# Output-weight load, down-weight splits, last value store and opening block of a fused attention and SwiGLU kernel

## The chip, the cores and the metric

The kernel runs on one core of a Trainium2 chip. The metric is the device time of one execution in microseconds. Three runs of the kernel before gave 1403.45, 1401.09 and 1399.49 us, median 1401.09 us. The profiler recorded one execution, which took 1402.34 us; its recorded span, to which every time of the trace belongs, is 1400.6 us.

## The reference

```python
def reference(A_x, A_wqkv, A_wo, B_x, B_w_gate, B_w_up, B_w_down):
    xn = _layernorm(A_x)                                   # x: [1, 2048, 512]
    q, k, v = (xn @ wqkv) as 3 x 32 heads x 16             # wqkv: [512, 1536]
    p = softmax(einsum("bhqd,bhkd->bhqk", q, k) * 16**-0.5)
    s = (p @ v) as [2048, 512] @ wo                        # wo: [512, 512]
    f = (silu(xn @ w_gate) * (xn @ w_up)) @ w_down         # 512 -> 1792 -> 512
    return A_x + s * silu(f)
```

All tensors are float32. The 2048 rows are both queries and keys, so 32 heads each need a 2048 x 2048 score matrix.

## The kernel before, in words

**Stages.** The prologue normalises x, multiplies by wqkv in four blocks of 512 rows and writes queries, keys and values to DRAM scratch (`q_d`, `k_d`, `v_d`). Its last stretch ends in a runtime branch (L801): a flag (L798) tells whether a cheap bound on the scores suffices. For the given data it does, and all five engines jump over the long general path. Then come attention with the feed-forward network (FFN) woven in, and an output projection with the final product.

**Attention.** The heads form 8 groups of 4, the queries 4 blocks of 512 rows: 32 units, each over 16 tiles of 128 keys. Keys and values of a group lie in a ring of four chunks of four tiles (`kst`, `vst`); chunks 0 and 1 have their memory before the branch, chunks 2 and 3 only after the prologue's pools are given back. PE multiplies one tile as two pairs of score matrices (L891), ACT takes their exponential (L894, L902), and one block later PE multiplies them with the values (`values`, L419). A block is a run of 2 to 6 key tiles of a unit. In some blocks, listed in `SHARED`, VectorE copies chosen half pairs out of PSUM (L899), and ACT takes their exponential from the copy at the end of the block (L912). A pair numbered n with sharing writes its second half into a PSUM bank of its own, `spare`; there is only one such bank, so each such copy has to end before the next shared pair's second half is written.

**The filling.** While ACT works, PE does FFN work in small steps, here called tokens: one token is a pair of 64-row matmuls into `bankx` and `banky` (L238). A feature tile has 24 tokens (gate with up), of which there are 7 in a group, followed by a down-projection of 4 times 21 tokens; 2 groups make a token block of 512 rows, and there are 4 of those. `fill(n)` issues n tokens behind a pair of scores. `plan()` chooses, by costs written in it, how many key tiles and how many tokens each block has, and its first entries are set by hand: `FIRST` gives the tokens ahead of the first pair and behind each pair of block 0.

**What rides on the tokens.** At a tile's first token VectorE splits the next tile's gate and up weights into two parts (`split_gu`, L198 and L199) and SP issues the loads of the tile after that. At its eighth token SP loads the tile's rows of the down weights into the only raw buffer, `wdr` (L204). At its last token VectorE forms the product (L268, L269), splits it (L230, L231), and `split_hidden` then splits the down weights (L208, L209). The output weights' rows use the same buffer `wdr` (`load_wo`, L302); the first of them is asked for at the last token of the last gate tile. SP issues its DMAs in program order: an issue that waits holds up all behind it.

**Order around the branch.** The last block of values is copied out of PSUM by ACT in four tiles (L714) into `vt` and stored to `v_d` by one DMA that SP issues behind the branch. SP then loads the ring's chunks 2 and 3, then the weights of gate tile 3 and the down weights of tile 1.

Of the kernel before, what the change touches and what calls it, by code (L numbers as in the profile page):

```python
# [25 lines left out]
NB = 4  # L26
TB = S // NB
NT = TB // P
# [11 lines left out]
DC = D // HALF  # L40
LIMIT = 160.0
SIZES = (2, 3, 4, 5, 6)
LAST = (3, 3, 3, 3, 2, 2)
FIRST = (4, 0, 4, 3, 3, 2, 2)
EARLY = 2


# [10 lines left out]
def plan():  # L58

    ends = [0]
    for i in range(2 * NB):
        nf = GROUPS[i % 2].stop - GROUPS[i % 2].start
        for n in [3 * DC] * nf + [3 * nf] * NT:
            ends.append(ends[-1] + n)

    ends = [n - ends[1] for n in ends[2:]]
    first = [(3, sum(FIRST)), (2, ends[0] - sum(FIRST))]
    units = H // 4 * NB
    start, stop = sum(k for k, _ in first), (units - 2) * KT
    pace = (ends[-1] - ends[0]) / (stop - start)
    short = lambda k, n: 15 * len(SHARED[k, n][0]) if (k, n) in SHARED else 250 * max(0, 6 * (k - 1) - n)
    ways = {at: {} for at in range(start, stop + 1)}
    ways[start][ends[0]] = 0, None
    for at in range(start, stop):
        room = KT - at % KT  # L80
        for done, (cost, _) in ways[at].items():
            rem = next((n for n in ends if n > done), done) - done
            for k in SIZES:
                for n in [rem] + list(range(3, rem - 2)):
                    to = at + k, done + n
                    if not n or n > 6 * k + 6 or k > room or room - k == 1:
                        continue
                    if abs(to[1] - ends[0] - (to[0] - start) * pace) > 45:
                        continue
                    c = cost + 327 + short(k, n) + (650 if n == rem and k == 2 else 0) + abs(n - 4.1 * k) / 2  # L90
                    if to[1] not in ways[to[0]] or ways[to[0]][to[1]][0] > c:
                        ways[to[0]][to[1]] = c, (at, done, k, n)

    rest = [3 * (DT - 1)] * EARLY
    pairs = {4: (2, 2), 5: (3, 2), 6: (3, 3)}
    cost = lambda r: ways[stop - r][ends[-1]][0] + sum(short(k, n) for k, n in zip(pairs[r], rest))
    r = min((r for r in pairs if ends[-1] in ways[stop - r]), key=cost)
    middle, step = [], ways[stop - r][ends[-1]][1]
    while step:
        middle.insert(0, step[2:])  # L100
        step = ways[step[0]][step[1]][1]
    rest += [3 * DT] * (NT * (NB - 1))
    parts = []
    for k, n in first + middle + list(zip(pairs[r] + 2 * LAST, rest)):
        m = 2 * k - 2
        even = [n // m + (i < n % m) for i in range(m)]
        shared, behind = SHARED.get((k, n), ((), even))
        parts.append((k, shared, [0, 0, *behind]))
    parts[0] = 3, (), list(FIRST[1:])
    return parts  # L110


# [1 line left out]
def tile_block(ctx: ExitStack, tc: tile.TileContext, x, wqkv, wo, w_gate, w_up, w_down, out):  # L114
# [3 lines left out]
    mm, act, dve, sp, pool = nc.tensor.matmul, nc.scalar.activation, nc.vector, nc.sync, nc.gpsimd  # L118
# [4 lines left out]
    v_d = dram.tile([NG, P, KT, VW], F32, name="v_d")  # L123
# [83 lines left out]
    def split_wd(f, i):  # L207
        dve.tensor_copy(wd[:, f, 0], wdr[i])  # L208
        dve.tensor_sub(wd[:, f, 1], wdr[i], wd[:, f, 0].bitcast(F32))  # L209
# [12 lines left out]
            after.pop(0)()  # L222


    kept = []

    def split_hidden():
        while kept:
            f, i, ga = kept.pop(0)
            dve.tensor_copy(hh[:, f, 0], ga)  # L230
            dve.tensor_sub(hh[:, f, 1], ga, hh[:, f, 0].bitcast(F32))  # L231
            split_wd(f, i)

    halves = [slice(h * HALF, (h + 1) * HALF) for h in range(2)]

# [11 lines left out]
    def ffn(b):  # L247
        for grp, part in enumerate(GROUPS):
            nf = part.stop - part.start
            for f in range(nf):  # L250
                i = b * NF + part.start + f
                if i + 1 < NB * NF:
                    split_gu(i + 1)
                if i + 2 < NB * NF:
                    load_gu(i + 2)
                hi, lo = gu.pop(i)
                n = 0
                for c in range(DC):
                    for wt, j in ((hi, 0), (hi, 1), (lo, 0)):
                        both(wt[:, c], fx[:, j, c], n == 0, n == 3 * DC - 1)  # L260
                        n += 1
                        if n == DC and i:
                            load_wd(i)
                        if n == 3 * DC:
                            th = one.tile([P, TB], F32, tag="th", name="th")
                            ga = two.tile([P, TB], F32, tag="ga", name="ga")
                            act(th, bankx, AF.Tanh, scale=0.5)  # L267
                            dve.scalar_tensor_tensor(ga, th, 1.0, bankx, op0=ALU.add, op1=ALU.mult)  # L268
                            dve.scalar_tensor_tensor(ga, ga, 0.5, banky, op0=ALU.mult, op1=ALU.mult)  # L269
                            kept.append((f, i, ga))  # L270
                            if now >= 0:
                                split_hidden()
                            if grp == 1 and f == nf - 1 and b + 1 < NB:
                                load_fx(b + 1, 0)
                                load_fx(b + 1, 1)
                            elif grp == 1 and f == nf - 1:
                                load_wo(0)
                        yield 3 * DC - n
            for t in range(NT):
                n = 0  # L280
                for f in range(nf):
                    for a, w in ((0, 0), (0, 1), (1, 0)):
                        both(hh[:, f, a, t * P:(t + 1) * P], wd[:, f, w], n == 0, n == 3 * nf - 1)
                        n += 1
                        if n == 3 * nf and grp == 0:
                            dve.tensor_copy(facc[:, t], bankx)
                            dve.tensor_add(facc[:, t], banky, facc[:, t])
                        elif n == 3 * nf:
                            y = two.tile([P, D], F32, tag="ga", name="y")
                            dve.tensor_add(y, bankx, facc[:, t])  # L290
                            dve.tensor_add(y, banky, y)
                            after.append(partial(store_gate, y, b * TB + t * P))
                            if b == NB - 1:
                                after.append(partial(next_out, t))
                        yield 3 * nf - n
# [4 lines left out]
    def load_wo(c):  # L300
        wor[c] = one.tile([P, D], F32, tag="wdr", name="wor")
        sp.dma_start(wor[c], wo[c * P:(c + 1) * P])  # L302
# [19 lines left out]
    plain, last, parts_o, lhs = [], [], {}, {}  # L322
# [156 lines left out]
    begin, n = [], 0  # L479
# [10 lines left out]
    with ExitStack() as pro:  # L490
# [74 lines left out]
        vt = plast.tile([P, NG, NT, VW], F32, name="vt")  # L565
# [120 lines left out]
        def feature_tile(b, m):  # L686
# [9 lines left out]
            if b:  # L696
                dve.tensor_max(top[m], top[m], sq)

        def value_tile(b, t):
            xh, xl = xt[b % 2]  # L700
            order = None
            if b == 0:
                parts = [slice(i, i + 1) for i in range(3)] if t == 1 else [slice(0, 3, 2), slice(1, 2)]
                order = [(i, part) for part in parts for i in range(DT)]
                if t == 1:
                    order.insert(11, (partial(turn_x, 0, 2), None))
            if b == t == 0:
                ps = first_tile()
            else:
                ps = project([(vh[:, c], vl[:, c], c) for c in range(DT)], xh, xl, slice(t * P, (t + 1) * P), order,  # L710
                             extra if b == t == NB - 1 else None)
            if b == 0 and t == 1:
                turn_x(0, 3)
            nc.scalar.copy(vt5[:, :, t, :, :DH], ps.rearrange("p (g h d) -> p g h d", g=NG, h=4))  # L714
            if t == NT - 1:
                store = partial((pool if b < NB - 1 else sp).dma_start, v_d[:, :, b * NT:(b + 1) * NT].rearrange("g p t c -> p g t c"), vt)
                if b < NB - 1:
                    store()
                return store


        def copy_fx(i):
# [78 lines left out]
        with tc.If(fast < 1):  # L801
            with tc.tile_pool(name="gen", bufs=1) as gen:
                for h in range(2):
                    pool.memset(qst[0][h * HALF:h * HALF + 2].bitcast(F32), 0.0)
                for g in range(NG):
                    for b in range(NB):
# [3 lines left out]
                        for j in range(NB):  # L810
                            load_k(g, j, j % 2)
                            for i in range(4 * NT):
                                h, t = divmod(i, NT)
# [36 lines left out]
    on = [att.tile([P, TB], F32, name=f"on{b}") for b in range(NB)]  # L850

    now = 0
    split_hidden()
    prev = None

    exps = []
# [2 lines left out]
    for u in range(units):  # L859
        g, b = divmod(u, NB)  # L860
        q = qst[u % 2]
        kt = 0
        for now in range(begin[u], begin[u + 1]):
            size, shared, parts = blocks[now]
# [4 lines left out]
            if not now:  # L869
                fill(FIRST[0])  # L870
            for n in range(2 * size):
                t, j = tiles[n // 2], n % 2
# [136 lines left out]
```

## Time and profile before

| what | before |
|---|---|
| runs, median | 1403.45, 1401.09, 1399.49 us; 1401.09 us |
| profiled execution, its span | 1402.34 us, 1400.6 us |
| PE busy | 1391.4 us (99% of the span) |
| ACT busy | 1109.6 us (79%) |
| VectorE (DVE) busy | 690.2 us (49%) |
| mean DMA rate | 107 GB/s |

A row of a timeline has the start in us, the duration in us, the engine (SPq is SP's queue of DMA issues), the line, the operation with its output and inputs, and in brackets the idle time ahead of it and what ended that. A row of the waits has the waiting instruction, what it waited for, the total in us, the number of times and the longest. A row of the windows has the window, its length, the busy time of PE, of PE's weight loads, DVE, ACT and POOL with the number of instructions, the granted TensorE clock as a share of full speed, the DMA engines' busy share and GB/s.

### The profile page before, as it was taken

Reading aid. Unit: us, or ns where it says so; the run is one execution under the profiler, and the core shown is the slowest. Engines: PE = TensorE matmul, PEld = TensorE weight load, DVE = VectorE, ACT = ScalarE, POOL = GpSimd, SP = SyncE. Lnnn points to the kernel's source line nnn. Section 1 sums busy time; section 2 is a strip of 40 time slices with the busy share of each in tenths; the row PEclk is TensorE's granted clock in tenths of the full one; section 3 lists DMA queues with packets and bytes.
Section 4 is the critical chain, followed back from the end, with each engine's and each line's share of the span. In section 5 each row is a group of like instructions: output and inputs, shape, how many; then the busy total and the mean of one; then the engine's idle time right before and its main releaser. Section 6 shows DMA issues by size and latency. Waiting matters only on the chain.

```text
span 1400.6 us, 27099 instructions
## 1 busy us (share of the span) xinstructions
PE 1391.4 (99%) x11197; PEld 832.3 (59%) x11197; DVE 690.2 (49%) x1121; ACT 1109.6 (79%) x1513; POOL 90.4 (6%) x102
## 2 busy tenths in 40 slices
PE   9999999999999999999999999999999999999998
PEld 7788655556555555565555555555555555555554
DVE  6643354254534563545356534644465435444645
ACT  6733588888888888887888888989888888878774
POOL 4200100000000000000000000000000000000254
PEclk9999999999999999999999999999999999999999
DMA  7778541134453511245524302447334212223643
GB/s 241 263 249 265 148 107 43 35 80 100 112 124 82 132 43 35 50 120 108 133 62 118 81 13 58 100 99 148 81 80 125 52 28 59 69 58 106 198 143 114
DMA packets 127648, 149.17 MB, mean 107 GB/s; under 512 B 12577, under 2 KB 79649, under 8 KB 126750
## 3 DMA queue, kind: packets, MB, share of 16 engines
q1 hardware_dynamic: 122206, 126.72, 35.8%
q0 software_dynamic: 4880, 20.12, 3.9%
q8 instruction: 90, 1.47, 0.4%
q10 hardware_dynamic: 432, 0.52, 0.1%
q14 instruction: 40, 0.33, 0.1%
HBM read 107.46 MB, written 40.11 MB: 105 GB/s over the span
## 4 chain that ended last, share of the span: by engine, by line
PE 86%; DMA 1%; DVE 1%; SPq 0%; ACT 0%; issue 0%; DVEq 0%
PE acc L419 32%; PE bankx L238 30%; PE score L891 18%; PE banky L238 6%; PE spare L891 1%; DMA wdr<-in_B_w_down_dram 1%; PE spare L947 0%; DMA kst<-k_d 0%; PE banky L947 0%; SPq L164 0%; PE score L947 0%; DVE ga L269 0%; DVE pr L899 0%; SPq L191 0%; DVE wd L208 0%
## 5 line engine op out<-in xcount | busy, mean ns | idle before, releaser
L894 ACT ACTIVATE pr<-score 128x1024 f32<-128x1024 f32 x746 | 725.6, 1028 | 101.7 <-PE score L891 90.3
L419 PE MATMUL acc<-pr,vst 128*17 128x512 f32 x4096 | 462.0, 593 | 0.0
L891 PE MATMUL score<-qst,kst 50*128 50x512 f32 x1770 | 408.3, 408 | 2.5 <-DMA kst<-k_d 2.5
L238 PE MATMUL bankx<-fx,guh 64*128 64x512 f32 x896 | 302.5, 393 | 0.1
L238 PE MATMUL banky<-fx,guh 64*128 64x512 f32 x896 | 302.2, 392 | 0.0
L891 PEld LDWEIGHTS score<-qst,kst 50*128 50x128 f32 x1770 | 195.7, 185 | 167.2 <-ACT pr L894 67.6
L419 PEld LDWEIGHTS acc<-pr,vst 128*17 128x17 f32 x4096 | 110.2, 97 | 279.8 <-issue 272.5
L899 DVE COPY pr<-spare 128x512 f32<-128x512 f32 x162 | 111.9, 690 | 247.7 <-PE spare L891 207.8
L902 ACT ACTIVATE pr<-score 128x512 f32<-128x512 f32 x219 | 130.7, 597 | 99.5 <-PE spare L891 90.0
L238 PE MATMUL bankx<-wd,hh 64*128 64x512 f32 x672 | 199.6, 396 | 0.0
L238 PE MATMUL banky<-wd,hh 64*128 64x512 f32 x672 | 199.3, 395 | 0.0
L238 PEld LDWEIGHTS bankx<-fx,guh 64*128 64x128 f32 x896 | 167.0, 187 | 28.5 <-issue 0.9
L238 PE MATMUL banky<-fx,gul 64*128 64x512 f32 x448 | 175.4, 392 | 0.0
L238 PE MATMUL bankx<-fx,gul 64*128 64x512 f32 x448 | 175.4, 392 | 0.0
L238 PEld LDWEIGHTS banky<-fx,guh 64*128 64x128 f32 x896 | 167.1, 187 | 3.9
L238 PEld LDWEIGHTS bankx<-wd,hh 64*128 64x128 f32 x672 | 126.7, 189 | 20.2
L268 DVE SCALAR_TENSOR_TENSOR ga<-th,bankx 128x512 f32<-128x512 f32 x56 | 38.5, 687 | 193.0 <-ACT th L267 193.0
L238 PEld LDWEIGHTS banky<-wd,hh 64*128 64x128 f32 x672 | 126.8, 189 | 4.1
L912 ACT ACTIVATE pr<-pr 128x512 f32<-128x512 f32 x221 | 121.1, 626 | 0.0
L891 PE MATMUL spare<-qst,kst 50*128 50x512 f32 x278 | 116.2, 418 | 0.7 <-DVE pr L899 0.6
L238 PEld LDWEIGHTS bankx<-fx,gul 64*128 64x128 f32 x448 | 83.0, 185 | 14.2
L238 PEld LDWEIGHTS banky<-fx,gul 64*128 64x128 f32 x448 | 83.0, 185 | 2.2
(171 smaller groups left out, 1402.2 us busy)
## 6 DMA issues: line engine op xcount, KB each, us to landing
gur<-in_B_w_gate_dram SPq DMA_DIRECT2D x56, 256.0 KB
gur<-in_B_w_up_dram SPq DMA_DIRECT2D x56, 256.0 KB
wdr<-in_B_w_down_dram SPq DMA_DIRECT2D x56, 256.0 KB
kst<-k_d SPq DMA_DIRECT2D x192, 64.0 KB
qst<-q_d SPq DMA_DIRECT2D x192, 64.0 KB
fx<-xt_d SPq DMA_DIRECT2D x24, 512.0 KB
q_d<-parts SPq DMA_DIRECT2D x16, 512.0 KB
k_d<-parts SPq DMA_DIRECT2D x16, 512.0 KB
```

The lines of the kernel that those rows point to most:

```text
L238: mm(bank, lhs[h], rhs[h], start=start, stop=stop)
L268: dve.scalar_tensor_tensor(ga, th, 1.0, bankx, op0=ALU.add, op1=ALU.mult)
L419: mm(acc[h * 32:h * 32 + DH + 1], v[:, kt % CT, h * (DH + 1):(h + 1) * (DH + 1)], probs[2 * i + h // 2][:, h % 2], start=kt == 0, stop=kt ...
L891: mm(spare if apart and h else room[:, h], k[r, j, kc * P:(kc + 1) * P], q[r, j], start=True, stop=True)
L894: exps.append(act(pr, room, AF.Exp, scale=0.25))
L899: dve.tensor_copy(pr[:, h], src)
L902: exps.append(act(pr[:, h], src, AF.Exp, scale=0.25))
L912: exps.append(act(part, part, AF.Exp, scale=0.25))
```

## The change

Four edits are made together.

1. `load_wo(0)` moves from the last token of the last gate tile to the eighth token of the last down-projection's first row tile.
2. The split of a tile's down weights moves out of `split_hidden` to the eighth token of the next tile (for tile 0 to the last token of tile 1, for a group's last tile to the eighth token of the down-projection that follows), and the load of the next rows goes right behind it. The product's split of tile 0, which stood at the head of the attention, moves to the end of tile 1.
3. The last block of values is stored by two DMAs: tiles 0 to 2 by one that stands ahead of the branch on SP, tile 3 by one behind it.
4. Unit 0 has blocks of 4, 6 and 6 key tiles with 20, 24 and 24 tokens, where it had 3, 2, 5 and 6 tiles with 14, 6, 24 and 24 tokens. The first of them shares pairs 4 and 7 with VectorE, the second is now of the shared kind. From unit 1 on the plan is the same.

```diff
-FIRST = (4, 0, 4, 3, 3, 2, 2)
+FIRST = (4, 0, 5, 2, 4, 1, 2, 3, 3)
...
-    first = [(3, sum(FIRST)), (2, ends[0] - sum(FIRST))]
+    first = [(4, ends[0])]
...
-    parts[0] = 3, (), list(FIRST[1:])
+    parts[0] = 4, (4, 7), list(FIRST[1:])
...
-    kept = []
+    kept, waiting = [], []
...
         while kept:
-            f, i, ga = kept.pop(0)
+            f, ga = kept.pop(0)
             dve.tensor_copy(hh[:, f, 0], ga)
             dve.tensor_sub(hh[:, f, 1], ga, hh[:, f, 0].bitcast(F32))
-            split_wd(f, i)
...
-                        if n == DC and i:
+                        if i and n == (DC if i > 1 else 3 * DC):
+                            while waiting:
+                                split_wd(*waiting.pop())
                             load_wd(i)
...
-                            kept.append((f, i, ga))
+                            kept.append((f, ga))
+                            waiting.append((f, i))
...
-                            elif grp == 1 and f == nf - 1:
-                                load_wo(0)
...
+                        if t == 0 and n == DC:
+                            split_wd(*waiting.pop())
+                            if grp == 1 and b == NB - 1:
+                                load_wo(0)
...
+        def store_v(engine, b, first, last):
+            dst = v_d[:, :, b * NT + first:b * NT + last].rearrange("g p t c -> p g t c")
+            engine.dma_start(dst, vt[:, :, first:last])
...
-            if t == NT - 1:
-                store = partial((pool if b < NB - 1 else sp).dma_start, v_d[:, :, b * NT:(b + 1) * NT].rearrange("g p t c -> p g t c"), vt)
-                if b < NB - 1:
-                    store()
-                return store
+            if b < NB - 1 and t == NT - 1:
+                store_v(pool, b, 0, NT)
+            elif b == NB - 1 and t == NT - 2:
+                store_v(sp, b, 0, t + 1)
+            elif b == NB - 1 and t == NT - 1:
+                return partial(store_v, sp, b, t, NT)
...
     now = 0
-    split_hidden()
     prev = None
```

**SP around the branch.** The program of SP has the store of the last values (`v_d<-vt`), the branch, and the end of the skipped path. Before, with the semaphores that a row waits for (the eight DMAHW ones count the landings of SP's DMAs):

```order
L798 TENSOR_LOAD flag_216 [waits DVE_49]
L798 ISA x2
L801 COMPARE_AND_BRANCH
...
L801 UNCONDITIONAL_BRANCH [waits DMAHW0_49,DMAHW1_49,DMAHW2_49,DMAHW3_49,DMAHW4_49,DMAHW5_49,DMAHW6_49,DMAHW7_49]
L833 DMA v_d_61<-vt_163 128x8x272 [waits DMAHW3_49,Activation_49]
```

And with the change:

```order
L807 TENSOR_LOAD flag_216 [waits DVE_49]
L807 ISA x2
L705 DMA v_d_61<-vt_163 128x8x204 [waits DMAHW3_49,Activation_49]
L810 COMPARE_AND_BRANCH
...
L810 UNCONDITIONAL_BRANCH [waits DMAHW0_49,DMAHW1_49,DMAHW2_49,DMAHW3_49,DMAHW4_49,DMAHW5_49,DMAHW6_49,DMAHW7_49]
L705 DMA v_d_61<-vt_163 128x8x68 [waits DMAHW4_49,Activation_49]
```

Three quarters of the store now stand ahead of the branch and wait for ACT's copy of the third value tile; the last quarter, in pieces of 68 numbers where a piece had 272, stands where the whole store stood. The wait for all eight counters of landings stands on the path that joins behind the branch; the skipped path's counts are added there too.

**VectorE in block 1 of the change.** In the rows of VectorE `pr<-spare` and `pr<-score` are the copies of shared pairs, `guh` and `gul` the split of a gate tile's weights, `wd` the split of down weights, `hh` the split of a product. Before, between the split of tile 1's product and the first copy of unit 0's last block:

```order
L230 CAST hh<-ga 128x512
L231 TENSOR_TENSOR hh<-ga,hh 128x512
L208 CAST wd<-wdr 128x512
L209 TENSOR_TENSOR wd<-wdr,wd 128x512
L198 CAST guh<-gur 128x1024
L199 TENSOR_TENSOR gul<-gur,guh 128x1024
L268 SCALAR_TENSOR_TENSOR ga<-th,bankx 128x512
```

With the change, from the same product of tile 1 on:

```order
L230 CAST hh<-ga 128x512
L231 TENSOR_TENSOR hh<-ga,hh 128x512
L907 COPY pr<-spare 128x512
L198 CAST guh<-gur 128x1024
L199 TENSOR_TENSOR gul<-gur,guh 128x1024
L907 COPY pr<-spare 128x512
L208 CAST wd<-wdr 128x512
L209 TENSOR_TENSOR wd<-wdr,wd 128x512
L907 COPY pr<-spare 128x512 x2
L907 COPY pr<-score_8967 128x512
```

The split of tile 3's weights (`guh`, `gul`) now stands between the copies of pairs 2 and 5 of the block, and the split of tile 1's down weights between those of pairs 5 and 7. The later rows of this kind are the same in every block of 6 tiles and 24 tokens that shares pairs: before, the copies of pairs 5, 7 and 9 followed each other, and the down weights were split ahead of the copy of pair 2.

**SP ahead of group 7's last key chunks.** `kst` is a key chunk, `vst` a value chunk, `wdr` the down weights' rows, `wor` the output weights'. Before:

```order
L204 DMA wdr<-in_B_w_down_dram 128x512
L302 DMA wor<-in_A_wo_dram 128x512
L164 DMA kst_8967<-k_d 16x2x512 x6
L181 DMA vst_8968<-v_d 128x272
L164 DMA kst_8971<-k_d 16x2x512 x6
```

With the change:

```order
L204 DMA wdr<-in_B_w_down_dram 128x512
L164 DMA kst_8968<-k_d 16x2x512 x6
L181 DMA vst_8969<-v_d 128x272
L164 DMA kst_8972<-k_d 16x2x512 x6
L181 DMA vst_8973<-v_d 128x272
L164 DMA qst_8976<-q_d 16x2x512 x6
L177 DMA qst_8976<-sh_d 2x2x512 x2
L306 DMA wor<-in_A_wo_dram 128x512 x2
```

The load of the output weights has gone from ahead of both chunks to behind them and behind the loads of the next unit's queries.

## The prediction

> **What bounds the kernel now.** First the page's busy times and its chain:
>
> ```profile
> PE 1391.4 (99%) x11197; PEld 832.3 (59%) x11197; DVE 690.2 (49%) x1121; ACT 1109.6 (79%) x1513; POOL 90.4 (6%) x102
> PE 86%; DMA 1%; DVE 1%; SPq 0%; ACT 0%; issue 0%; DVEq 0%
> ```
>
> PE is busy in 1391.4 of 1400.6 us. None of the edits takes a matmul away, so each can win only what PE idles (9.2 us in all) or what it runs at a low clock, and each can lose by making PE wait. Two places of the trace have such losses: the last key chunks of group 7 and the opening of the attention. The first is seen in SP's queue, its waits, and PE:
>
> ```profile
> 1226.43 0.35 SPq L204 DMA_DIRECT2D wdr<-in_B_w_down_dram  x1
> 1240.40 0.33 SPq L302 DMA_DIRECT2D wor<-in_A_wo_dram  x1
> 1240.83 2.71 SPq L164 DMA_DIRECT2D kst<-k_d  x6
> ```
> ```profile
> SPq L302 <- DVE wd L209: 11.3, 1, 11.3
> ```
> ```profile
> 1245.36 0.47 PE L891 MATMUL score<-qst,kst 50*128 50x512 f32 x1 [2.04 <-DMA kst<-k_d]
> 1246.26 0.76 PE L891 MATMUL score<-qst,kst 50*128 50x512 f32 x1 [0.43 <-DMA kst<-k_d]
> ```
>
> The output weights' load waits 11.3 us for the buffer, the key load queued behind it starts at 1240.83, and PE idles 2.04 and 0.43 us for it. The windows show what follows. First the block with this stall and one of the same size (5 tiles, 21 tokens); then the stretch of the idle time, and the next:
>
> ```profile
> 1235.82:1254.34 18.52, 16.05 (x112) 9.78 (x112) 6.14 (x11) 11.61 (x17) 0.00 (x0) 0.82 0.35 94
> 1094.40:1107.19 12.79, 12.79 (x112) 7.17 (x112) 5.60 (x9) 11.51 (x18) 0.00 (x0) 1.00 0.00 1
> ...
> 1242.32:1245.72 3.40, 1.36 (x11) 0.67 (x7) 0.59 (x1) 1.38 (x2) 0.00 (x0) 1.00 0.71 189
> 1245.73:1252.55 6.82, 6.39 (x31) 5.39 (x32) 0.37 (x1) 3.67 (x4) 0.00 (x0) 0.50 0.48 127
> ```
>
> After a stretch of 3.40 us in which PE worked 1.36 us, the granted clock is 0.50 for 6.82 us. Half a clock over 6.82 us costs about 3.4 us; with the idle 2.47 us that is nearly the 5.73 us by which the block exceeds its like. The opening is the second place: the four blocks of unit 0, then a block of 6 tiles with sharing behind one of 4, and one behind one of 6:
>
> ```profile
> 157.29:162.55 5.26, 5.26 (x42) 3.57 (x39) 0.00 (x0) 4.74 (x6) 0.03 (x1) 1.00 0.63 213
> 162.55:168.15 5.60, 5.60 (x46) 2.59 (x46) 4.88 (x6) 4.20 (x7) 4.53 (x4) 1.00 0.44 109
> 168.15:178.12 9.97, 9.97 (x87) 7.22 (x84) 4.20 (x7) 9.92 (x14) 0.00 (x0) 1.00 0.73 168
> 178.12:192.64 14.52, 13.82 (x115) 7.75 (x111) 9.87 (x15) 10.18 (x15) 0.00 (x0) 1.00 0.67 146
> 853.25:865.55 12.30, 12.30 (x106) 7.36 (x106) 7.27 (x12) 10.35 (x15) 0.00 (x0) 1.00 0.26 58
> 865.55:879.43 13.88, 13.88 (x123) 7.96 (x121) 8.71 (x13) 12.38 (x19) 0.00 (x0) 1.00 0.26 57
> ```
>
> Unit 0 takes 35.35 us (157.29 to 192.64).
>
> **The change part by part.** The sum is made against the profiled execution, 1402.34 us, and put on the median of the runs, 1401.09 us, which lies 1.25 us below.
>
> **Edit 1, output weights: -5.8 us.** With the load gone from ahead of the keys, they queue behind the last `wdr` load only. That load now waits for a split at its tile's eighth token, in the place where VectorE stood at about 1230 to 1232, so the keys start near 1232 and come some 8 us ahead of need. The block then takes what its kind takes, 12.7 to 12.8 us: 18.52 less 12.75 is 5.8. The output weights themselves are asked for after the last chunk; nothing needs them before the output projection's first split, a down-projection later. If the half clock came from something else, only 2.5 us would be won.
>
> **Edit 4, the opening, first without waits.** Block 0 has 8 pairs of scores and 20 tokens behind them (four tokens stand ahead, as before). The 6 pairs and 14 tokens of before took 5.26 us, 0.26 each; 28 of these make 7.0 to 7.3. Blocks 1 and 2 are the kinds of the last two rows above, 12.30 and 13.9 to 14.0. That is 33.3 us, 2.1 less than 35.35. To this the waits are added, and there are two.
>
> **Edit 3, the store in two parts.** SP before, and the copies by ACT that it waits for:
>
> ```profile
> 156.79 0.40 SPq L833 DMA_DIRECT2D v_d<-vt  x1
> 162.45 2.67 SPq L164 DMA_DIRECT2D kst<-k_d  x6
> ...
> 169.95 0.67 SPq L191 DMA_DIRECT2D gur<-in_B_w_gate_dram  x1
> 170.68 0.61 SPq L191 DMA_DIRECT2D gur<-in_B_w_up_dram  x1
> 171.40 0.56 SPq L204 DMA_DIRECT2D wdr<-in_B_w_down_dram  x1
> ```
> ```profile
> SPq L164 <- DMA v_d<-vt: 4.7, 1, 4.7
> SPq L801 <- SPq L801: 4.4, 1, 4.4
> ```
> ```profile
> 153.38 0.59 ACT L714 COPY vt<-ps 128x512 f32<-128x512 f32 x1 [2.40 <-PE ps L641]
> 156.18 0.59 ACT L714 COPY vt<-extra 128x512 f32<-128x512 f32 x1 [2.21 <-PE extra L641]
> ```
> ```profile
> 157.29 0.67 PE L891 MATMUL score<-qst,kst 50*128 50x512 f32 x4
> ```
>
> SP's branch costs it 4.4 us. Before, that lay beside the projection of the last value tiles: SP had nothing to do until ACT's copy ended at 156.77. Now part 1 stands ahead of the branch and waits for the third copy, 153.97. SP branches at about 154.4, is through at 157.4 (a branch of 3 us) to 158.8, and then waits on the eight counters for part 1's landing as well. The whole store took from 156.79 to 162.4 to land; three quarters of it, begun at 154.0, land between 158.2 (in proportion) and 159.6. PE's first scores wait for these counters too. So they start between 158.2 and 159.6 instead of 157.29: 0.9 to 2.3 us of idle PE, say 1.6. Part 2 is issued about 159 instead of 156.79. It holds a quarter of the bytes in as many pieces, so it lands after 1.4 us (by bytes) to 5.6 us (by pieces): at 160.4 to 164.6 where before it was 162.4. I take 163, near the middle and nearer the pieces, since the pieces are what stays the same. The prologue's memory, and with it the ring's key loads, comes free 0.5 us later rather than earlier.
>
> [...]
>
> **Who waits for that: VectorE, then PE.** The loads of tile 3's weights (169.95, 170.68) and tile 1's down weights (171.40) come behind twelve key issues, 7.5 to 9 us after the ring starts. VectorE before shows when the last of them landed and what the splits take:
>
> ```profile
> 176.38 0.43 DVE L208 CAST wd<-wdr 128x512 fp32r<-128x512 f32 x1 [4.46 <-DMA wdr<-in_B_w_down_dram]
> 176.84 0.69 DVE L209 TENSOR_TENSOR wd<-wdr,wd 128x512 fp32r<-128x512 f32 x1
> 177.45 0.69 DVE L198 CAST guh<-gur 128x1024 fp32r<-128x1024 f32 x1
> 178.17 1.23 DVE L199 TENSOR_TENSOR gul<-gur,guh 128x1024 fp32r<-128x1024 f32 x1
> ```
>
> The down weights landed at 176.38, so tile 3's, issued 0.7 us ahead of them, at about 175.5. Before, only VectorE felt this (4.46 us), for its block shared nothing. In the changed order the split of tile 3 stands ahead of the copy of pair 5, and PE may not write pair 7's second half before that copy ends. Landing 175.5 + 0.5 (later ring), splits 1.9, copy 0.7: pair 7 cannot go on before about 178.6. PE comes there 8.4 us into the block (7 pairs, 3.4 us of values, 12 tokens): at 157.29 + 7.0 + 8.4 = 172.7 without the first wait, 174.3 with it. So PE waits about 4.3 us there, and with the first wait 5.9 us in all, or 5.9 whether the first is 0.9 or 2.3, as long as the ring start is the same. Pair 9 then follows the split of the down weights closely, which adds up to 0.5. Unit 0: 33.3 + 6.2 = 39.5 us against 35.35, **+4.2 us**; with part 2's ends (160.4 or 164.6) +1.6 to +5.9.
>
> **The clock after that wait: +3.4 us.** More than 4 us without a matmul, with a stretch of 3.4 us in which PE works less than 1.36 us, is what halved the clock at 1245.73. I expect the same here: another 3.4 us, unless the first wait does it (then the slow time ends inside the second wait and costs little).
>
> [...]
>
> **Edit 2, splits beside the next tile.** VectorE and PE in one of the 26 later blocks of 6 tiles that share:
>
> ```profile
> 226.85 0.68 DVE L899 COPY pr<-spare 128x512 f32<-128x512 f32 x1
> 228.35 0.69 DVE L899 COPY pr<-spare 128x512 f32<-128x512 f32 x1 [0.82 <-PE spare L891]
> ```
> ```profile
> 229.30 0.39 PE L891 MATMUL spare<-qst,kst 50*128 50x512 f32 x1
> ```
>
> The copies of pairs 5 and 7 start at 226.85 and 228.35, with 0.82 us of idle time between; the split (0.43 and 0.69, 1.07 in a chain) now lies there. Pair 7's copy starts at 226.85 + 0.61 + 1.07 = 228.53 instead of 228.35 and ends at 229.22, 0.08 ahead of pair 9's second half at 229.30. A semaphore's way and the weight load use most of that. So nothing (0 us) to 0.1 us a block; I take 0.04, **+1.0 us** for 26. Elsewhere the moved splits fall in idle time: VectorE is busy 49%. If that cover were gone, each would cost its 1.07 us.
>
> **Sum:** -5.8 + 4.2 + 3.4 + 1.0 = +2.8 us: 1405.1 for a profiled execution like the one of before, 1403.9 on the median. I say 1404.0.
>
> **The rivals.**
> *A. The opening waits, but the late clock stays whole* (the first wait of up to 2.3 us in one stretch halves it instead, and the slow time runs into the second wait; or neither does). For: the first wait reaches 2.04 us in a third to half of its range. Against: its middle is 1.6. -5.8 + 4.2 + 1.0 = -0.6: 1400.5.
> *B. It does what it says.* Part 2 lands near 160.4 or the weights land sooner behind a less loaded queue, and PE waits for nothing in the opening: -5.8 - 2.1 + 0.5 = -7.4: 1393.7. Against it stands the twelve-issue queue ahead of tile 3's weights: even a ring start 2 us earlier only takes 2 us from a wait of 4.3.
> *C. Slower by the splits.* If pair 7's copy comes too late in each of the 26 blocks (it decides at about 0.06 us ahead of the matmul, which the rows leave open with 0.08), PE loses about 0.12 us a block and the weight load's cover: 3.1 instead of 1.0, on top of the forecast: 1406.1. For: the lead is small and the same in all 26 blocks. Against: by the rows it is just enough.
>
> **How the numbers follow.** Forecast 0.45 (1404.0, own range 1401 to 1406), A 0.31 (1400.5, from 1398 with an early part 2 to 1402), B 0.10 (1393.7), C 0.14 (1406.1, up to 1408). The range that leaves out B and the outermost ends of the others is 1397.5 to 1408. About 0.3%, 4.2 us, is what a measurement of this kernel can tell from no change: faster is below 1396.9, slower above 1405.3. Faster: B and little of A, 0.11. Slower: C and 0.2 of the forecast's upper end, 0.34. The rest, 0.55, is no change.
>
> **What would show it.** Right: no DMA wait and a clock of 1.00 near 1240; PE's first score at 158.2 to 159.6; PE waiting about 4 us for VectorE's copy (`spare`) some 8 us into block 1, behind a DVE wait for `gur`; half a clock after it; blocks of 6 shared tiles 0 to 0.1 us longer. Wrong: key loads of the ring starting before 161, no `spare` wait in block 1, or a clock of 1.00 all through 157 to 190.

## The result, and the profile after

In 20 runs of each, the changed kernel took 1402.45 us (1400.47 to 1404.90) and the kernel before 1400.53 us (1397.39 to 1403.45), both medians. The ratio is 1.0012, with a 95% interval of 1.0005 to 1.0019: 0.7 to 2.7 us slower. The forecast was 1404.0 us, by a sum of +2.8 us. The profiled execution took 1403.09 us, its span is 1401.3 us. Lines of code are numbered anew in the change: the scores are L899 now, the copies L907, the last store L705.

On the page PE works as long as before, in a span 0.7 us longer; the busy times of the other engines have moved by less than 2 us, that of the weight loads (PEld) by 7.6:

```profile
PE 1391.3 (99%) x11197; PEld 839.9 (60%) x11197; DVE 691.6 (49%) x1128; ACT 1109.4 (79%) x1517; POOL 89.5 (6%) x102
```

**Group 7's last keys.** SP's queue in the change (this part of the program runs 6.8 us later than before), and the block that took 18.52 us before:

```profile
1239.20 0.35 SPq L204 DMA_DIRECT2D wdr<-in_B_w_down_dram  x1
1239.65 4.14 SPq L164 DMA_DIRECT2D kst<-k_d  x6
...
1251.07 10.43 SPq L306 DMA_DIRECT2D wor<-in_A_wo_dram  x2
```
```profile
1242.63:1255.32 12.69, 12.69 (x112) 7.42 (x112) 6.13 (x11) 11.42 (x18) 0.00 (x0) 1.00 0.46 123
```

The keys go out right behind the `wdr` load, the output weights wait behind them, PE never idles and the clock is 1.00. The block takes 12.69 us: 5.8 us are won.

**The opening.** SP, PE's two waits, and VectorE ahead of the second of them:

```profile
154.50 5.78 SPq L705 DMA_DIRECT2D v_d<-vt  x2
163.62 2.67 SPq L164 DMA_DIRECT2D kst<-k_d  x6
...
170.07 0.67 SPq L191 DMA_DIRECT2D gur<-in_B_w_gate_dram  x1
170.78 0.63 SPq L191 DMA_DIRECT2D gur<-in_B_w_up_dram  x1
171.87 0.62 SPq L204 DMA_DIRECT2D wdr<-in_B_w_down_dram  x1
```
```profile
160.05 1.37 PE L899 MATMUL score<-qst,kst 50*128 50x512 f32 x4 [2.07 <-SPq L810]
179.22 0.50 PE L899 MATMUL spare<-qst,kst 50*128 50x512 f32 x1 [1.90 <-DVE pr L907]
```
```profile
176.62 0.69 DVE L198 CAST guh<-gur 128x1024 fp32r<-128x1024 f32 x1 [2.48 <-DMA gur<-in_B_w_up_dram]
177.34 1.23 DVE L199 TENSOR_TENSOR gul<-gur,guh 128x1024 fp32r<-128x1024 f32 x1
178.49 0.68 DVE L907 COPY pr<-spare 128x512 f32<-128x512 f32 x1
```

The row of the two stores runs from the first part's issue to the end of the second's: the branch lies in its 5.78 us. PE waits 2.07 us for SP's branch (L810): SP spends 3.9 us on the branch itself and then 0.4 us on the landing of part 1. Later VectorE waits for tile 3's weights, and the copy of pair 5, queued behind their split, ends at 179.17; PE had to have that bank free and goes on at 179.22. The windows show what each wait did to the clock (first five rows), and then the three blocks of unit 0 (last three rows):

```profile
156.92:160.33 3.41, 1.34 (x10) 0.83 (x11) 1.29 (x2) 0.34 (x1) 0.00 (x0) 1.00 0.39 118
160.34:163.75 3.41, 3.41 (x17) 3.17 (x18) 0.00 (x0) 1.94 (x2) 0.08 (x1) 0.50 0.37 84
163.76:167.16 3.40, 3.40 (x29) 2.73 (x27) 0.69 (x1) 3.08 (x4) 3.24 (x4) 1.00 0.49 110
177.40:180.81 3.41, 1.58 (x12) 1.11 (x12) 3.38 (x5) 0.90 (x3) 0.00 (x0) 1.00 0.35 99
180.82:184.23 3.41, 3.41 (x18) 2.69 (x18) 1.05 (x3) 1.96 (x3) 0.00 (x0) 0.50 1.10 223
160.05:168.63 8.58, 8.58 (x56) 7.19 (x58) 1.19 (x2) 6.49 (x8) 3.78 (x4) 0.80 0.46 108
168.63:184.83 16.20, 14.30 (x106) 8.60 (x106) 10.78 (x18) 11.02 (x16) 0.00 (x0) 0.89 0.80 176
184.83:198.99 14.16, 14.16 (x124) 8.55 (x120) 8.62 (x13) 12.28 (x19) 0.00 (x0) 1.00 0.19 47
```

Behind each wait the clock is halved for one stretch of 3.41 us. The two halved stretches begin 20.48 us apart (160.34 and 180.82), which is six times 3.41. Unit 0 ends at 198.99, before at 192.64; 0.51 us of the difference was there ahead of the opening (the third copy of values began at 153.89 instead of 153.38). The opening thus lost 5.84 us, as much as edit 1 won. So the gain of edit 1 near 1240 is there in full, and it had been given away beforehand, between 157 and 199.

### The profile page after: what moved, and what is told of

The parts are those of the page before. It is cut to its first block, busy times and chain, and to the rows that moved or that the text cites. A ratio compares the mean times of both kernels' runs of the same rounds, so it can differ in the third digit from the quotient of the medians.

```text
span 1401.3 us, 27070 instructions
## 1 busy us (share of the span) xinstructions
PE 1391.3 (99%) x11197; PEld 839.9 (60%) x11197; DVE 691.6 (49%) x1128; ACT 1109.4 (79%) x1517; POOL 89.5 (6%) x102
## 4 chain that ended last, share of the span: by engine, by line
PE 87%; SPq 0%; DMA 0%; DVE 0%; issue 0%; DVEq 0%
PE acc L423 32%; PE bankx L237 29%; PE score L899 18%; PE banky L237 7%; PE spare L899 1%; DMA gur<-in_B_w_up_dram 0%; SPq L164 0%; PE spare L955 0%; PE banky L955 0%; PE score L955 0%; DVE gul L199 0%; SPq L181 0%; DVE guh L198 0%; DVE y L962 0%; SPq L191 0%
## 5 line engine op out<-in xcount | busy, mean ns | idle before, releaser
L899 PE MATMUL score<-qst,kst 50*128 50x512 f32 x1766 | 408.8, 408 | 2.1 <-SPq L810 2.1
L899 PEld LDWEIGHTS score<-qst,kst 50*128 50x128 f32 x1766 | 195.3, 185 | 162.9 <-ACT pr L902 67.3
L907 DVE COPY pr<-spare 128x512 f32<-128x512 f32 x167 | 115.0, 689 | 257.4 <-PE spare L899 212.9
L920 ACT ACTIVATE pr<-pr 128x512 f32<-128x512 f32 x228 | 125.2, 631 | 0.0
L899 PE MATMUL spare<-qst,kst 50*128 50x512 f32 x282 | 118.8, 421 | 1.9 <-DVE pr L907 1.9
```

The source lines that it names most:

```text
L899: mm(spare if apart and h else room[:, h], k[r, j, kc * P:(kc + 1) * P], q[r, j], start=True, stop=True)
L907: dve.tensor_copy(pr[:, h], src)
L920: exps.append(act(part, part, AF.Exp, scale=0.25))
```

## The experiments

All times are medians; ratios are to the kernel before, run on the same chip beside each, with 95% intervals.

| kernel | edits in it | median us | ratio, interval |
|---|---|---|---|
| the change | 1, 2, 3, 4 | 1402.45 | 1.0012, 1.0005 to 1.0019 |
| wo_only | 1 | 1395.25 | 0.9958, 0.9945 to 0.9972 |
| one_store | 1, 2, 4 | 1402.30 | 1.0011, 1.0002 to 1.0020 |
| old_opening | 1, 2, 3 | 1399.21 | 0.9986, 0.9977 to 0.9995 |
| one_store_old_opening | 1, 2 | 1395.77 | 0.9965, 0.9953 to 0.9978 |
| early_gate | all, tile 3's weights earlier | 1398.48 | 0.9985, 0.9976 to 0.9994 |
| both_behind | all, both stores behind the branch | 1402.85 | 1.0019, 1.0010 to 1.0028 |
| weights_first | 1, 2, 4, loads in another order | 1395.28 | 0.9964, 0.9949 to 0.9978 |
| weights_first_two_parts | the same, both stores behind the branch | 1395.96 | 0.9967, 0.9956 to 0.9979 |
| wo_only_again | 1 | 1395.08 | 0.9962, 0.9948 to 0.9976 |
| weights_first_again | as weights_first | 1394.94 | 0.9959, 0.9945 to 0.9973 |

The theory: edit 1 wins 5.8 us; the opening loses them again in two waits of PE, one from the store ahead of the branch (edit 3) and one from the shared copies queued behind the split of weights that come late (edit 4), each with a stretch of halved clock. The rivals: the half clock near 1245 had another cause; or one of the two waits is only the other's consequence.

**Edit 1 alone (wo_only).**

```diff
-                            elif grp == 1 and f == nf - 1:
-                                load_wo(0)
...
+                        if t == 0 and n == DC and grp == 1 and b == NB - 1:
+                            load_wo(0)
```

> The kernel before with edit 1 alone: the output weights' load behind the last keys, all else as before. Theory: the wait of 2.5 us and the half clock that it brings both go, so the block that took 18.52 us takes 12.7, and the kernel runs 5.5 to 6 us faster than before (ratio near 0.996). Rival: the half clock there has another cause (a DMA burst, say) and stays; then only the wait of 2.5 us comes back (ratio near 0.998).

The ratio is 0.9958, so 5.9 us faster (3.9 to 7.7). The block in question, in windows of this kernel, and two stretches of its opening:

```profile
1236.98:1249.67 12.69, 12.69 (x112) 7.13 (x112) 6.14 (x11) 11.43 (x18) 0.00 (x0) 1.00 0.16 44
...
184.72:188.13 3.41, 2.02 (x17) 1.47 (x17) 2.36 (x5) 2.06 (x3) 0.00 (x0) 1.00 0.23 42
188.14:191.55 3.41, 2.84 (x26) 2.02 (x24) 2.47 (x3) 1.86 (x3) 0.00 (x0) 1.00 0.30 97
```

The block is 5.83 us shorter, with the whole clock. The rival that gave the half clock another cause is out; a burst of DMAs alone did not halve it in weights_first, below, where the DMA engines are busy 0.99 of block 0 at a clock of 1.00. The second pair of rows is of use further down: PE idled 1.39 us of a stretch here, and the clock stayed whole.

**One store (one_store): edit 3 undone.**

```diff
-            elif b == NB - 1 and t == NT - 2:
-                store_v(sp, b, 0, t + 1)
             elif b == NB - 1 and t == NT - 1:
-                return partial(store_v, sp, b, t, NT)
+                return partial(store_v, sp, b, 0, NT)
```

> The changed kernel with edit 3 undone: one store of the last values behind the branch. Theory (two waits, each with a stretch of halved clock): PE's first score comes right behind its four tokens, no clock is lost in block 0, the ring's keys start about 1.2 us earlier; the wait at pair 7 of block 1 stays and is longer, 4 to 5 us, since PE comes there earlier and the weights of tile 3 still land behind twelve key loads. Unit 0 ends 1 to 2 us earlier than with the change. Rival (the branch is what costs, the wait at pair 7 is only its consequence): with the first wait gone block 1 runs without a wait above 1 us and unit 0 ends 5 us or more earlier.

The time is that of the change (1.0011 against 1.0012). SP and PE of this kernel (its scores are L897, its copies L905), and its windows: blocks 0 and 1, then the stretches of the wait.

```profile
156.86 0.40 SPq L705 DMA_DIRECT2D v_d<-vt  x1
162.23 2.67 SPq L164 DMA_DIRECT2D kst<-k_d  x6
```
```profile
178.45 0.79 PE L897 MATMUL spare<-qst,kst 50*128 50x512 f32 x1 [5.38 <-DVE pr L905]
```
```profile
157.38:164.38 7.00, 7.00 (x58) 4.98 (x56) 1.37 (x3) 6.41 (x8) 1.97 (x3) 1.00 0.56 186
164.38:184.08 19.70, 14.31 (x107) 8.72 (x105) 11.32 (x18) 10.70 (x16) 1.98 (x2) 0.83 0.75 172
...
171.94:175.35 3.41, 1.13 (x9) 0.57 (x7) 0.00 (x0) 1.65 (x3) 0.00 (x0) 1.00 1.01 222
175.36:182.18 6.82, 3.73 (x18) 2.94 (x20) 4.42 (x7) 1.51 (x2) 0.00 (x0) 0.50 0.81 192
```

The first wait is gone and block 0 takes 7.00 us; then PE waits 5.38 us for the same copy, more than the 4 to 5 expected. It comes to that place at 173.07, with the change at 177.32: its first score is 2.67 us later there and block 0 takes 1.58 us longer. So with the change it waited less, and the second wait is no consequence of the first: it takes up the time that the first one costs. The release of the ring at 162.23 instead of 163.62 moved the copy by only 0.8 us. Unit 0 ends 0.87 us earlier than with the change, where 1 to 2 us were expected; behind this longer wait the half clock lasts 6.82 us instead of 3.41.

**The old opening (old_opening): edit 4 undone.** `FIRST` and the first blocks as before; edits 1 to 3 stay.

> The changed kernel with edit 4 undone: unit 0 in blocks of 3, 2, 5 and 6 tiles again, edits 1 to 3 kept. Theory: the first wait of about 2 us and its half clock stay (they are edit 3's), and there is no wait for a copy in the 5-tile block, which shares nothing; unit 0 ends 2 to 4 us later than before, so with the 5.8 us of edit 1 the kernel is 2 to 3.5 us faster than before. Rival (edit 4's blocks are themselves the better opening, with or without waits): it is not faster than the changed kernel.

It is 2.0 us faster than before by the ratio (0.7 to 3.2), the lower end of what was expected. PE's first score, then the stretch of the wait and the next, block 0 and unit 0's last block:

```profile
159.61 0.93 PE L899 MATMUL score<-qst,kst 50*128 50x512 f32 x4 [1.92 <-SPq L810]
```
```profile
157.59:161.00 3.41, 1.49 (x13) 1.32 (x12) 0.27 (x1) 0.61 (x1) 0.00 (x0) 1.00 0.27 66
161.01:164.41 3.40, 3.40 (x18) 2.40 (x17) 1.12 (x1) 2.72 (x4) 1.17 (x2) 0.50 0.24 60
159.61:166.30 6.69, 6.69 (x41) 4.98 (x41) 1.82 (x2) 5.04 (x6) 3.01 (x3) 0.74 0.35 91
181.85:194.93 13.08, 13.08 (x114) 8.08 (x111) 8.62 (x13) 10.07 (x15) 0.00 (x0) 1.00 0.44 104
```

The first wait and its half clock are edit 3's: 1.92 us, and block 0 is 1.43 us longer than the 5.26 of before. No wait for a copy follows. The rival (the new blocks are the better opening, waits or not) is out: this kernel is faster than the change (0.9986 against 1.0012).

**Both undone (one_store_old_opening): edits 1 and 2 alone.**

> Edits 1 and 2 alone: one store behind the branch and the opening of 3, 2, 5 and 6 tiles. Theory: no wait at the first score, no halved clock; unit 0 ends no later than before, and up to 1.4 us earlier, since the last block of unit 0 takes 13.1 us instead of 14.5 without the split of down weights ahead of its first copy; with 5.8 us of edit 1 it is 6 to 7 us faster than before (ratio 0.9950 to 0.9957). Rival (edit 2 costs in the later blocks what it saves): equal to edit 1 alone within 0.5 us.

In the profile no wait of PE is left in unit 0, and the span is 6.8 us shorter than before, as expected. Unit 0's last block:

```profile
177.96:191.12 13.16, 13.16 (x115) 7.87 (x111) 9.56 (x15) 10.18 (x15) 0.00 (x0) 1.00 0.52 132
```

The timed runs give 0.9965, 4.9 us faster (3.1 to 6.6), less than the 6 to 7 expected and edit 1 alone within what they can tell. So the rival has the number, and its reason in part: from unit 1 to group 7's last keys this kernel takes 0.7 us longer than before, while the 1.4 us that its last block of unit 0 seems to save (13.16 against 14.52) are saved by edit 1 alone as well in another execution (last experiment). From the four kernels with edits 1 and 2, in ratios times 1400.5: edit 3 alone costs 2.9 us (0.9986 less 0.9965), edit 4 alone 6.4 (1.0011 less 0.9965), the two together 6.6 (1.0012 less 0.9965), each uncertain by about 2 us. The profiled spans give 3.9, 6.9 and 7.6. They don't add up, because the one wait hides in the other.

**Tile 3's weights earlier (early_gate).**

```diff
+    load_gu(3)
     for c in range(2, NB):
         load_k(0, c)
...
-                if i + 2 < NB * NF:
+                if i + 2 < NB * NF and i + 2 not in gu:
```

> The changed kernel with one load moved: the weights of gate tile 3 are asked for ahead of the ring's key chunks, behind the store's second part. Theory: the split of tile 3 is done long before pair 5, the wait of 1.9 us at pair 7 and the half clock behind it go, the down weights of tile 1 come just in time for pair 9; unit 0 ends 3 to 4 us earlier than with the change. Rival (the time at pair 7 is set by the down weights or by the key chunks, not by tile 3): the wait moves to pair 9 and unit 0 ends less than 1.5 us earlier.

The ratio is 0.9985, 3.8 us below the change. Its windows: the stretch of the first wait and the next, then block 1.

```profile
156.37:159.78 3.41, 1.68 (x11) 1.23 (x13) 1.19 (x1) 0.29 (x1) 0.00 (x0) 1.00 0.39 118
159.79:163.19 3.40, 3.40 (x18) 3.11 (x18) 0.00 (x0) 2.03 (x3) 0.00 (x0) 0.50 0.78 172
...
167.78:180.29 12.51, 12.51 (x106) 7.62 (x106) 10.69 (x18) 10.82 (x16) 0.00 (x0) 1.00 0.66 173
```

One tile's gate and up weights, asked for ahead of the ring's keys, take block 1 from 16.20 to 12.51 us, and unit 0 from 38.94 to 34.90. The second wait was tile 3's weights; the down weights did not take their place, which was the rival.

**Both parts behind the branch (both_behind).**

```diff
-            elif b == NB - 1 and t == NT - 2:
-                store_v(sp, b, 0, t + 1)
             elif b == NB - 1 and t == NT - 1:
-                return partial(store_v, sp, b, t, NT)
+                return lambda: (store_v(sp, b, 0, t), store_v(sp, b, t, NT))
```

> The changed kernel with both parts of the last value store behind the branch, nothing else altered. Theory: the first wait came from the part ahead of the branch, so it goes and block 0 takes 7.0 us at full clock; the ring's keys start near 161, a little earlier than with one store (162.2), since only the last quarter waits for the last copy. The wait at pair 7 of block 1 (weights of tile 3) stays, 4 to 5 us with two halved stretches; the time stays within 1.5 us of the changed kernel. Rival (small pieces are what is slow): the ring's keys start later than with one store, at 163 or after, and the time is above the changed kernel's.

```profile
154.99 2.12 SPq L705 DMA_DIRECT2D v_d<-vt  x2
162.32 2.67 SPq L164 DMA_DIRECT2D kst<-k_d  x6
```

As expected the first wait goes and the time stays; the second wait is 5.62 us, against 4 to 5 expected. But the ring's keys start at 162.32 and not near 161: splitting the store wins nothing. Part 2, issued at about 156.7 (the pair of rows ends at 157.11, and an issue takes 0.4), releases the keys 5.6 us later; the whole store, with four times its bytes in as many pieces, took 5.4 us in one_store. In the change, where part 1 had landed before, part 2 took 3.7 us (issued at 159.9, keys at 163.62). The theory was wrong in that one number.

The records of the DMA packets show why. With the change the 1024 packets of part 2, of 272 B, take 19 ns each and run from 160.82 to 162.14, 1.3 us in all. In one_store the 1024 packets of the whole store, of 1088 B, take 51 ns each and run from 157.79 to 161.31, 3.5 us. So fewer bytes did make shorter packets here. But 2.4 us with the change and 1.9 us in one_store lie outside the packets, 0.9 us of it in each from the issue to the first packet. And in both_behind part 2's packets begin at 158.50 while part 1's still run (to 160.13), and end at 161.34, 2.8 us later: the same number of pieces that took 1.3 us alone. So part 2 lost its time beside part 1, and the number of pieces does not tell it. In bytes per ns the small ones were the slowest: 272 B in 19 ns are 14 B per ns, 816 B (part 1 with the change) in 41 ns 20, and 1088 B in 51 ns 21.

**All loads in another order (weights_first).** One store, tile 3's weights ahead of the ring, and the ring's last chunk behind block 0, so that tile 1's down weights are asked for ahead of it.

```diff
-    for c in range(2, NB):
-        load_k(0, c)
-        load_v(0, c)
+    load_gu(3)
+    load_k(0, 2)
+    load_v(0, 2)
...
+            if not now:
+                load_k(0, 3)
+                load_v(0, 3)
```

> The changed kernel with one store behind the branch, the weights of gate tile 3 asked for ahead of the ring's keys, and the ring's last chunk behind block 0, so that the down weights of tile 1 are asked for ahead of it. Theory: all waits of the opening are gone; unit 0 takes 33.3 to 34 us at full clock (7.0, 12.3, 14.0), 1.5 to 2 us less than before, and with edit 1 the kernel is 7 to 8 us faster than before (ratio 0.9943 to 0.9950). Rival (the down weights still come behind pair 7's copy, or the key chunk 2 comes too late for pair 8): a wait of 1 to 3 us in block 1, and no gain over edit 1 alone.

```profile
157.00:164.01 7.01, 7.01 (x59) 4.99 (x56) 1.55 (x3) 6.41 (x8) 1.50 (x2) 1.00 0.99 248
164.01:176.52 12.51, 12.51 (x106) 7.58 (x106) 10.75 (x18) 10.80 (x16) 2.45 (x3) 1.00 0.59 150
176.52:190.44 13.92, 13.92 (x122) 8.38 (x121) 8.62 (x13) 12.36 (x19) 0.00 (x0) 1.00 0.55 117
```

Unit 0 takes 33.44 us without a wait, and the span is 1393.0 us, 7.6 below before's. In the timed runs it is 5.0 us faster than before (3.1 to 7.1), less than was expected and no more than edit 1 alone.

**The same with the store in two parts (weights_first_two_parts).**

> As the kernel with the weights first, but the store in two parts, both behind the branch. Theory: the same as with one store within 0.5 us, since nothing on PE's path waits for the ring's start any more. Rival (the ring's start still sets PE's time through the down weights or chunk 2): it differs by the shift of the ring's start, about 1 us.

0.9967 against 0.9964: no difference, as expected. PE waits nowhere in unit 0 in this profile, though the ring's keys start 0.9 us later (163.17 against 162.26).

**Edit 1 and the weights first, side by side.**

> Edit 1 alone once more, on the same chip as the kernel with the weights first, to compare the two directly: in the profiled executions they lie 2.7 us apart (spans 1395.7 and 1393.0), in the timed runs, from two chips, not at all (medians 1395.25 and 1395.28). If the waits that the profile shows in unit 0 of edit 1 alone (1.4 and 0.6 us) are there in every execution, its median is 2 to 3 us above the other's. If they belong to the profiled execution, the medians agree within 0.7 us.

> The kernel with the weights first, beside edit 1 alone on the same chip: 2 to 3 us faster than that if unit 0's waits are in every execution, equal within 0.7 us if they belong to the profiled one.

Medians 1395.08 (1394.68 to 1395.85) and 1394.94 us (1394.82 to 1395.66), both profiled spans 1392.9 us. They are equal. In the second profile of edit 1 alone VectorE waits 0.39 us for the second down weights, where its first profile had 2.92 and the kernel before 2.32:

```profile
181.91 0.43 DVE L208 CAST wd<-wdr 128x512 fp32r<-128x512 f32 x1 [0.39 <-DMA wdr<-in_B_w_down_dram]
```

Unit 0 takes 33.9 us there (156.90 to 190.81), in the first profile of the same kernel 36.6. So the waits of the old opening hang on how soon these weights land, and differ between executions.

## Why the prediction was right, point by point

- **Edit 1, -5.8 us: right.** -5.83 in the profile; edit 1 alone is 5.9 us faster by the runs and shows the cause. The keys started where the prediction had them (near 1232; 1239.65 less the 6.8 us by which all was late).
- **The opening without waits, 33.3 us: right.** 33.44 in weights_first.
- **The first wait, 0.9 to 2.3 us, taken as 1.6: right in place and cause**, at the upper end in size (2.07, 1.92 and 1.67 in the three kernels with a store ahead of the branch). The wait was SP's branch and then part 1's landing, as said. The ring was released near 163, also as said, but that is in part luck: the forecast leaned to the time of the whole store because the number of pieces stays the same, while part 2's 3.7 us are 1.3 us of packets and 2.4 us around them.
- **The second wait, 4.3 us: right in place and cause, mis-sized.** The bank came free at 179.2, against the 178.6 of the prediction on a trace 0.5 us earlier. PE waited 1.90 us in that row, because the first wait had already halved the clock: block 0 took 1.57 us longer (8.58 less 7.01), and the first wait was 0.5 us longer than taken, so PE came that much later to a bank that was free no sooner. Without either, in one_store, it waited 5.38 us.
- **The clock, +3.4 us after the second wait: mis-sized, by about half.** The step expected one halving of 6.82 us, as in the trace of before, after the second wait or after the first. The runs show one after each wait, of 3.41 us each. The first cost little beyond the waits, since its 1.57 us came off the second wait; the second cost 1.8 us (block 1's 14.30 us of PE work against 12.51 in early_gate). The opening as a whole lost 5.84 us, where 7.6 were forecast (4.2 and 3.4). The case thus lies between the forecast and rival A, and so does the time: 1402.45 between 1404.0 and 1400.5. The step's "less than 1.36 us" of work in such a stretch came from the one case it had; in the change the clock was halved behind 1.34 us of work and behind 1.58.
- **Edit 2, +1.0 us: too much.** In the change the copy of pair 7 ends 0.12 us ahead of the matmul:

```profile
233.23 0.68 DVE L907 COPY pr<-spare 128x512 f32<-128x512 f32 x1
233.83 0.42 DVE L208 CAST wd<-wdr 128x512 fp32r<-128x512 f32 x1
234.28 0.69 DVE L209 TENSOR_TENSOR wd<-wdr,wd 128x512 fp32r<-128x512 f32 x1
234.89 0.68 DVE L907 COPY pr<-spare 128x512 f32<-128x512 f32 x1
```
```profile
235.69 0.43 PE L899 MATMUL spare<-qst,kst 50*128 50x512 f32 x1
```

  That was enough: a matmul that had to wait for such a copy began 0.05 us behind its end in the change (179.17, 179.22) and 0.06 us in the kernel before (188.50, 188.56). The 26 blocks of its kind took 0.28 us more than before in sum, in the other kernels with edit 2 0.13 to 0.39, and in the two profiles without it (edit 1 alone) -0.06 and 0.22 us. All blocks together from unit 1 to group 7's last keys took 0.5 to 0.8 us more than before with edit 2, and -0.2 and 0.1 without. Rival C, which needed 0.12 us a block, is out.
- **The reference of the sum, and some luck.** In the profiled pair the terms come to +1.0 us (-5.83, +5.84, 0.5 for edit 2 in all later blocks, and the 0.5 us ahead of the opening that no term had), and the spans differ by 0.7; the forecast's +2.8 was 2 us too much for that pair. The runs differ by 1.9. The profiled execution of the kernel before was 1.8 us above its median, that of the change 0.6 above its own. The kernel before had 35.35 us in unit 0 there, of which edit 1 alone needs only 33.9 in another execution; that can account for the difference, but only one execution of the kernel before was profiled, so it is not shown. The prediction took that wait as a fixed part of the kernel before. That 1402.45 came so near to 1404.0 is in part this luck.
- **Rival B** (no waits in the opening) was refuted for the change; it holds once the weights are asked for ahead of the keys.

Left open is why the down weights of the old opening land sooner in some executions than in others; no run here tells.

## What to carry to other kernels

When a schedule gives an engine a new job in a stretch, look up what else stands in that engine's queue there: late weights did little harm while VectorE alone waited for them; here copies that PE needs stood behind them, and PE waited too (1.90 us). Two waits of the same engine that follow each other need not add up (here 2.9 us and 6.4 us alone, 6.6 together), so undoing one of them may show nothing; undo them one by one and together. And look at a wait of PE for two prices, its length and a halved clock behind it: the second wait of the change cost 1.90 us and then 1.8 us by the clock, while behind 1.39 us of idle time in a stretch of wo_only the clock stayed whole.

## What the runs showed of the hardware that was not expected

What is said here of the clock was measured in the traces of these runs. Each row has a stretch of 3.40 or 3.41 us by the windows, PE's work in it, and the granted clock behind it:

| run | stretch | PE's work, us | clock behind it |
|---|---|---|---|
| before | 1242.32:1245.72 | 1.36 | 0.50 for 6.82 us |
| the change | 156.92:160.33 | 1.34 | 0.50 for 3.41 us |
| the change | 177.40:180.81 | 1.58 | 0.50 for 3.41 us |
| one_store | 171.94:175.35 | 1.13 | 0.50 for 6.82 us |
| old_opening | 157.59:161.00 | 1.49 | 0.50 for 3.40 us |
| early_gate | 156.37:159.78 | 1.68 | 0.50 for 3.40 us |
| both_behind | 173.57:176.98 | 0.00 | 0.50 for 6.82 us |
| wo_only | 184.72:188.13 | 2.02 | 1.00 |
| wo_only | 188.14:191.55 | 2.84 | 1.00 |

In the four rows with 3.40 or 3.41 us of half clock PE was busy all through it. In the three with 6.82 us PE was not busy all through the first 3.41 us of it: it worked 2.98 us of them in the kernel before, 0.31 us in one_store and 1.81 us in both_behind, whose stretch ahead had no work at all:

```profile
173.57:176.98 3.41, 0.00 (x0) 0.00 (x0) 0.97 (x2) 0.03 (x1) 0.00 (x0) 1.00 1.07 220
176.99:183.81 6.82, 5.23 (x24) 4.17 (x26) 3.85 (x6) 1.65 (x3) 0.00 (x0) 0.50 0.80 173
```

Half of PE's work under the half clock is an estimate of what it cost on top of the wait itself: 1.7 us for a stretch of 3.41 us with PE busy throughout (1.57 us were measured in block 0 of the change, 1.8 in block 1), and 3.2, 1.9 and 2.6 us in the kernel before, one_store and both_behind, where PE worked 6.39, 3.73 and 5.23 us of the 6.82. The rows are what these traces show, and no more.
